# Reordering the DMA transposes on one queue of a fused cross-attention and maxout-FFN kernel

## The chip, the cores and the metric

The kernel runs on one core of a Trainium2 chip. A core has five engines, each with its own in-order instruction queue: PE (TensorE, matrix multiplication), DVE (VectorE), ACT (ScalarE), POOL (GpSimd) and SP (SyncE, which computes nothing and here issues transfers). They wait for one another by semaphores. The metric is the device time of one execution in microseconds; lower is better.

## What is computed

The reference first does a cross-attention between 512 tokens x and 32 states of each of 8 batches and 8 heads, in both directions, and then sends all 8 * (512 + 32) rows through a maxout layer and an output projection:

```python
def _attn_ref(x, state):                      # x: 8,8,512,64   state: 8,8,32,64
    scores = scale * np.matmul(x, state.transpose(0, 1, 3, 2))
    ...                                       # softmax over the 32 states -> a
    xread = np.matmul(a, state)
    scores2 = scale * np.matmul(state, x.transpose(0, 1, 3, 2))
    ...                                       # softmax over the 512 tokens -> a2
    sread = np.matmul(a2, x)
    return np.concatenate([xread, sread], axis=2)

def _moe_ref(x, w1, w2, w3, w_out):           # x: 4352,512   w: 512,768   w_out: 768,512
    h = np.maximum(np.maximum(x @ w1, x @ w2), x @ w3)
    return h @ w_out
```

Inputs and output are float32; the kernel multiplies in bfloat16.

## The kernel before

The work goes batch by batch, 0 to 7, and the stages of several batches are interleaved. For one batch b the names of the stages, which are also the names in the plan below, are these:

- `lx` (line 201): POOL's queue loads x of the batch, 512 KB, into a buffer of its own. `pad` (line 375) copies it on POOL into a padded layout.
- `xtd` (`x_turn_dma`, line 291): SP issues a DMA transpose of x, written to the tile xT.
- `sc` (line 305): PE multiplies xT with the states: the scores. `ex` (line 313): ACT takes the exponential, tile e. `sum` (lines 342 and 344): DVE sums it and takes reciprocals. `wt` (line 349): POOL multiplies e by the reciprocals, tile a, the attention weights.
- `atd` (`a_turn_dma`, line 366): SP issues a DMA transpose of a, written to the tile aT. There are three buffers for aT.
- `sr` (line 391): PE makes the state reads (the sread of the reference). `srs` (line 407): DVE scales them, tile sr. `srt` (`sread_turn`, line 410): SP issues a DMA transpose of them into the batch's own slice of the tile ats. `ap` (`sread_place`, line 415): a copy, on ACT unless the plan says otherwise, from that slice into the tile atp. Only the layer-1 work on the state rows, `l1s`, near the end of the kernel, reads atp.
- `gr`, `gq` (line 427) and `grc`, `gqc` (lines 466 and 469): PE multiplies the states with the three weight matrices, and ACT or DVE copies the result to the tile G. With G, layer 1 is one product with the attention weights.
- `l1 b m` (line 477): PE multiplies aT by G, for slice m (0 to 5) of the 768 hidden units, into three PSUM banks, one for each weight matrix. `m0` (line 492, ACT), `ma` (line 497, DVE) and `mb` (line 505, DVE) take the maximum of the three and so free the three banks.
- `l2 b j` (line 514): PE does the output projection of 128 tokens. `l2c` (line 526): ACT or DVE copies it out of PSUM. `so` (line 548): a queue stores it.

The order is written out by hand. The string PLAN (line 18) is a list of such operations, a function `perform` (line 615) goes through it once and emits the instructions, and each engine runs its own instructions in the order in which they are emitted, each waiting for the data and buffers that it needs. The letters D, A, P and S name the engine or queue. Two operations on different engines that change places in the list change nothing in either engine's own order. BANKS gives the PSUM bank of each operation in the order of the list, for those operations that take one; PLACES gives the buffer of each tile. Of the operations that the change moves, none takes a bank.

In the plan, from batch 2 on, one pass of the loop does the layer 1 of batch b and prepares batch b + 1. SP's queue holds, in the passes of b = 2 to 5, `xtd` of batch b + 2, `srt` of b - 2 and `atd` of b + 1, in this order; the pass of b = 6 has no `xtd`. In the pass of b = 2 that is `xtd 4`, `srt 0`, `atd 3`. `atd` is followed by `ap` of b - 2 on ACT, at the end of the pass, just ahead of `grc`, the copies of the next but one batch's G.

Of the kernel before, what the change touches and what calls it, by code (L numbers as in the profile page):

```python
# [34 lines left out]
    so 0 0 2 P; lx 4; m0 1 5; l2 0 2; ma 1 5; mb 1 5; stp 3 A; l2c 0 2 A; l2 1 0; gq 2 1024 1280; gr 3 0 512;  # L35
    gr 3 1792 2304; l2c 1 0 D; grc 3 1792 2304 D; gqc 2 1024 1280 A; grc 3 0 512 A; atd 2; sr 2; l2 1 1; srs 2;
    sc 3 -; l1 2 0; m0 2 0; ex 3 -; l2c 1 1 D; l2 1 3; ma 2 0; gq 3 1024 1280; so 0 2 4 P; gqc 3 1024 1280 A;
    l2c 1 3 A; gr 3 512 1024; gr 3 1280 1792; mb 2 0; xtd 4; sum 3 -; sr 3; srs 3; l1 2 1; m0 2 1; ma 2 1;
    l1 2 2; m0 2 2; mb 2 1; ma 2 2; l1 2 3; m0 2 3; mb 2 2; srt 0; ma 2 3; l1 2 5; wt 3 - P; m0 2 5; mb 2 3;
    l2 1 2; grc 3 1280 1792 A; grc 3 512 1024 A; ma 2 5; mb 2 5; l2c 1 2 D; l1 2 4; so 1 2 4 P; m0 2 4; ma 2 4;  # L40
    lx 5; mb 2 4; atd 3; ap 0 A; so 1 0 2 P; pad 4; gr 4 1792 2304; gr 4 0 512; grc 4 1792 2304 AD; l2 2 0;
    l2 2 1; grc 4 0 512 D; l2c 2 0 A; l1 3 0; m0 3 0; sc 4 -; ex 4 -; xtd 5; l2c 2 1 D; l2 2 3; ma 3 0;
    gq 4 1024 1280; gr 4 1280 1792; gr 4 512 1024; mb 3 0; sr 4; gqc 4 1024 1280 A; sum 4 -; srs 4; l2c 2 3 A;
    l1 3 1; m0 3 1; ma 3 1; l1 3 2; m0 3 2; mb 3 1; ma 3 2; l1 3 3; m0 3 3; mb 3 2; srt 1; ma 3 3; l1 3 5;
    wt 4 - P; m0 3 5; mb 3 3; l2 2 2; grc 4 1280 1792 A; grc 4 512 1024 A; ma 3 5; mb 3 5; l2c 2 2 D; l1 3 4;
    so 2 2 4 P; m0 3 4; ma 3 4; lx 6; mb 3 4; atd 4; ap 1 A; so 2 0 2 P; pad 5; gr 5 1792 2304; gr 5 0 512;
    grc 5 1792 2304 AD; l2 3 0; l2 3 1; grc 5 0 512 D; l2c 3 0 A; l1 4 0; m0 4 0; sc 5 -; ex 5 -; xtd 6;
    l2c 3 1 D; l2 3 3; ma 4 0; gq 5 1024 1280; gr 5 1280 1792; gr 5 512 1024; mb 4 0; sr 5; gqc 5 1024 1280 A;
    sum 5 -; srs 5; l2c 3 3 A; l1 4 1; m0 4 1; ma 4 1; l1 4 2; m0 4 2; mb 4 1; ma 4 2; l1 4 3; m0 4 3; mb 4 2;
    srt 2; ma 4 3; l1 4 5; wt 5 - P; m0 4 5; mb 4 3; l2 3 2; grc 5 1280 1792 A; grc 5 512 1024 A; ma 4 5;  # L50
    mb 4 5; l2c 3 2 D; l1 4 4; so 3 2 4 P; m0 4 4; ma 4 4; lx 7; mb 4 4; atd 5; ap 2 A; so 3 0 2 P; pad 6;
    gr 6 1792 2304; gr 6 0 512; grc 6 1792 2304 AD; l2 4 0; l2 4 1; grc 6 0 512 D; l2c 4 0 A; l1 5 0; m0 5 0;
    sc 6 -; ex 6 -; xtd 7; l2c 4 1 D; l2 4 3; ma 5 0; gq 6 1024 1280; gr 6 1280 1792; gr 6 512 1024; mb 5 0;
    sr 6; gqc 6 1024 1280 A; sum 6 -; srs 6; l2c 4 3 A; l1 5 1; m0 5 1; ma 5 1; l1 5 2; m0 5 2; mb 5 1; ma 5 2;
    l1 5 3; m0 5 3; mb 5 2; srt 3; ma 5 3; l1 5 5; wt 6 - P; m0 5 5; mb 5 3; l2 4 2; grc 6 1280 1792 A;
    grc 6 512 1024 A; ma 5 5; mb 5 5; l2c 4 2 D; l1 5 4; so 4 2 4 P; m0 5 4; ma 5 4; mb 5 4; atd 6; ap 3 A;
    so 4 0 2 P; pad 7; gr 7 1792 2304; gr 7 0 512; grc 7 1792 2304 AD; l2 5 0; l2 5 1; grc 7 0 512 D; l2c 5 0 A;
    l1 6 0; m0 6 0; sc 7 -; ex 7 -; l2c 5 1 D; l2 5 3; ma 6 0; gq 7 1024 1280; gr 7 1280 1792; gr 7 512 1024;
    mb 6 0; sr 7; gqc 7 1024 1280 A; sum 7 -; srs 7; l2c 5 3 A; l1 6 1; m0 6 1; ma 6 1; l1 6 2; m0 6 2; mb 6 1;
    ma 6 2; l1 6 3; m0 6 3; mb 6 2; srt 4; ma 6 3; l1 6 5; wt 7 - P; m0 6 5; mb 6 3; l2 5 2; grc 7 1280 1792 A;  # L60
    grc 7 512 1024 A; ma 6 5; mb 6 5; l2c 5 2 D; l1 6 4; so 5 2 4 P; m0 6 4; ma 6 4; mb 6 4; atd 7; ap 4 A;
    so 5 0 2 P; srt 6; l1 7 0; srt 7; m0 7 0; l2 6 0; ap 7 D; srt 5; ma 7 0; mb 7 0; l1 7 2; m0 7 2; ap 6 A;
    l2c 6 0 D; ma 7 2; l1 7 3; m0 7 3; ap 5 A; mb 7 2; ma 7 3; l1 7 4; m0 7 4; l2 6 1; l2c 6 1 A; ma 7 4;
    mb 7 4; l1s 0; m0 s 0; l2 6 2; l2c 6 2 A; look; ma s 0; mb s 0; so 6 2 3 S; mb 7 3; l1 7 1; m0 7 1; ma 7 1;
    l1s 2; m0 s 2; mb 7 1; ma s 2; l1 7 5; m0 7 5; mb s 2; ma 7 5; l1s 1; m0 s 1; ma s 1; so 6 0 1 S; mb 7 5;
    l1s 5; m0 s 5; l2p 7 2 384 512; ma s 5; mb s 1; mb s 5; l1s 3; m0 s 3; l2pc 7 2 384 512 A; l2p 7 0 384 512;
    l2p 7 3 256 512; sop 7 2 384 512 P; ma s 3; l2p 7 2 128 384; mb s 3; l2p 7 0 0 128; l2pc 7 0 0 128 A;
    l2pc 7 3 256 512 D; l2p 7 1 0 128; l2pc 7 0 384 512 D; l2p 7 3 0 256; flag; l2pc 7 1 0 128 A;
    l2pc 7 2 128 384 A; l1s 4; m0 s 4; l2 6 3; sop 7 0 0 128 P; ma s 4; sop 7 0 384 512 P; mb s 4;
    l2p s 0 256 512; so 6 1 2 P; l2 s 1; sop 7 3 256 512 A; l2c 6 3 D; l2p 7 2 0 128; sop 7 1 0 128 S;  # L70
    so 6 3 4 A; l2pc 7 3 0 256 D; l2p s 0 0 256; l2pc s 0 256 512 D; sop s 0 256 512 A; l2pc 7 2 0 128 A;
    l2p 7 1 128 384; sop 7 2 0 128 A; l2p 7 0 256 384; l2pc s 0 0 256 A; l2pc 7 1 128 384 A; l2c s 1 D;
    l2p 7 1 384 512; l2p 7 0 128 256; sop 7 3 0 256 S; sop 7 2 128 384 P; l2pc 7 0 256 384 D; sop 7 1 128 384 A;
# [670 lines left out]
```

## Time and profile before

| | us |
|---|---|
| median of 3 runs | 152.40 |
| lowest and highest of them | 151.75, 153.13 |
| the profiled execution, its own time | 153.36 |
| its span, from first to last instruction | 151.6 |

In the profile's rows, a line number and the tile names say which operation a row is: `aT<-a` at L366 is `atd`, `xT<-x` at L291 is `xtd`, `ats<-sr` at L410 is `srt`, `atp<-ats` at L415 is `ap`. A row of a timeline has the start in us, the duration in us, the engine, the line, the operation, the tiles, and the number of instructions merged; in square brackets stand the engine's idle time before it and what ended that. "SPq" rows are the times at which SP's queue issues a transfer; when it lands is told separately, counted from its issue. "PEld" is the loading of weights into PE, which overlaps with its multiplications. A row of busy times in stretches gives, after the stretch, its length, then busy time and number of instructions of PE, PEld, DVE, ACT and POOL, the clock granted to PE, the DMA engines' share and their GB/s.

### The profile page before, as it was taken

The page shows a single profiled execution, that of the slowest core. Times are in us where ns is not written, and L with a number is a line of the kernel's source. Part 1 is how long each engine was busy: PE and PEld are TensorE (multiplying, and loading weights), DVE is VectorE, ACT ScalarE, POOL GpSimd, SP SyncE. Part 2 cuts the span into 40 slices and gives each one's busy share as a digit, 9 for nine tenths or more (in the row PEclk, how much of TensorE's full clock was granted, in tenths as well). Part 3 has the DMA queues.
Part 4 walks back from the last instruction along what each step waited for, and adds up shares of the span by engine and source line. Part 5 has one row for each costly group of instructions (what it writes and reads, how often), then busy time and mean ns, then how long its engine had stood idle before and what let it go on. Part 6 is the DMA issues. An engine that isn't in the chain of part 4 may idle for free.

```text
span 151.6 us, 3618 instructions
## 1 busy us (share of the span) xinstructions
PE 145.2 (96%) x1422; PEld 72.6 (48%) x1422; DVE 118.5 (78%) x202; ACT 83.2 (55%) x144; POOL 56.1 (37%) x78
## 2 busy tenths in 40 slices
PE   6998999999999999899999999999999999999991
PEld 2555443335444443444344435443544446689770
DVE  6488788999967895789978997899779887675443
ACT  3366888966655574466646664666466653332220
POOL 6996911081491508250555055405340200001500
PEclk9999999999999999999999999999999999999999
DMA  4999999959668978996589659965403240300555
GB/s 132 173 182 190 201 232 198 186 113 127 109 145 161 225 152 211 98 215 132 168 100 235 126 163 119 231 129 157 183 4 78 103 191 6 138 0 17 188 202 162
DMA packets 39108, 22.29 MB, mean 147 GB/s; under 512 B 23072, under 2 KB 36896, under 8 KB 39088
## 3 DMA queue, kind: packets, MB, share of 16 engines
q0 software_dynamic: 15872, 13.96, 48.9%
q1 hardware_dynamic: 21632, 6.69, 22.5%
q10 hardware_dynamic: 1584, 1.38, 3.0%
q8 instruction: 12, 0.20, 0.6%
q14 instruction: 8, 0.07, 0.2%
HBM read 15.20 MB, written 8.91 MB: 159 GB/s over the span
## 4 chain that ended last, share of the span: by engine, by line
PE 84%; DMA 8%; POOL 2%; DVE 2%; issue 1%; ACT 1%; POOLq 0%; SPq 0%; DVEq 0%
PE pw L477 46%; PE po L514 22%; PE pg L427 5%; DMA w<-in_moe_w_dram 5%; PE po L532 4%; DMA aT<-a 3%; PE ps L305 2%; PE psr L391 2%; POOL w L217 1%; POOL x L206 1%; PE pgh L427 1%; ACT G L444 1%; PE pt L261 1%; DVE ht L505 0%; DVE t L497 0%
## 5 line engine op out<-in xcount | busy, mean ns | idle before, releaser
L477 PE MATMUL pw<-aT,G 128*128 128x512 bf16 x288 | 66.7, 379 | 0.8 <-DMA aT<-a 0.8
L492 ACT CAST t<-pw 128x512 bf16<-128x512 f32 (+1 forms) x54 | 30.4, 564 | 28.2 <-PE pw L477 25.2
L497 DVE TENSOR_TENSOR t<-t,pw 128x512 bf16<-128x512 bf16 (+1 forms) x54 | 35.3, 655 | 11.0 <-ACT t L492 8.8
L477 PEld LDWEIGHTS <-G 128*128 128x128 bf16 x288 | 27.1, 98 | 33.7 <-issue 3.2
L514 PE MATMUL po<-wout,ht 128*128 128x512 bf16 x168 | 39.7, 379 | 0.0
L505 DVE TENSOR_TENSOR ht<-t,pw 128x512 bf16<-128x512 bf16 x48 | 33.0, 687 | 4.5
L349 POOL TENSOR_TENSOR a<-e,rden 128x1024 bf16<-128x1024 bf16 (+1 forms) x9 | 14.5, 1619 | 27.6 <-ACT osb L526 12.0
L514 PEld LDWEIGHTS <-ht 128*128 128x128 bf16 x168 | 15.4, 98 | 19.0 <-issue 1.7
L548 POOL DMA_DIRECT2D out_dram<-osb x13 | 7.5, 576 | 27.5 <-ACT t L492 27.5
L466 ACT CAST G<-pg 128x1024 bf16<-128x1024 f32 (+1 forms) x17 | 14.7, 901 | 1.5 <-PE pg L427 1.5
L526 ACT COPY osb<-po 128x512 f32<-128x512 f32 x15 | 8.9, 591 | 8.1 <-PE po L514 8.1
L466 DVE CAST G<-pg 128x1024 bf16<-128x1024 f32 (+1 forms) x12 | 11.6, 997 | 1.3 <-ACT G L466 1.2
L526 DVE COPY osb<-po 128x512 f32<-128x512 f32 x14 | 9.6, 687 | 3.6 <-PE po L514 3.5
L375 POOL COPY xp<-x 128x1024 bf16<-128x1024 bf16 x12 | 12.3, 1064 | 0.0
L313 ACT ACTIVATE e<-ps 128x1024 bf16<-128x1024 f32 (+1 forms) x10 | 8.5, 853 | 6.8 <-PE ps L305 6.8
L342 DVE TENSOR_REDUCE seen<-e 128x32 f32<-128x1024 bf16 (+1 forms) x10 | 10.0, 998 | 1.6 <-ACT e L313 1.6
L427 PE MATMUL pg<-w,bd 64*32 64x512 bf16 (+1 forms) x288 | 10.7, 362 | 0.4 <-ACT G L444 0.2
L444 ACT CAST G<-pg 128x768 bf16<-128x768 f32 x10 | 8.0, 810 | 2.7 <-PE pg L427 2.5
L543 POOL DMA_DIRECT2D out_dram<-osb x4 | 2.2, 541 | 19.4 <-ACT osb L537 19.4
L249 PE MATMUL idle<-zero 128*128 128x512 bf16 x18 | 7.4, 503 | 1.8 <-DVE zero L225 1.3
L477 PE MATMUL pw<-atp,w 128*128 128x256 bf16 x72 | 8.7, 272 | 0.0
L217 POOL DMA_DIRECT2D w<-in_moe_w_dram x10 | 7.7, 780 | 0.1
(70 smaller groups left out, 112.7 us busy)
## 6 DMA issues: line engine op xcount, KB each, us to landing
out_dram<-osb POOLq DMA_DIRECT2D x12, 512.0 KB, 3.7
x<-in_x_dram POOLq DMA_DIRECT2D x4, 512.0 KB, 7.5
x<-in_x_dram POOLq DMA_DIRECT2D x7, 256.0 KB, 5.9
w<-in_moe_w_dram POOLq DMA_DIRECT2D x4, 256.0 KB, 7.8
w<-in_moe_w_dram POOLq DMA_DIRECT2D x2, 384.0 KB, 8.0
wout<-in_moe_w_out_dram POOLq DMA_DIRECT2D x1, 768.0 KB, 12.6
out_dram<-osb SPq DMA_DIRECT2D x3, 256.0 KB, 2.4
stf<-in_state_dram ACTq DMA_DIRECT2D x4, 128.0 KB, 5.3
```

Of the source, the lines that this page charges most:

```text
L342: nc.vector.reduce_sum(out=den, in_=parity(e[b], g), axis=AX.X)
L349: times[c](out=parity(a[b], g).rearrange("p j g s n -> p j (g s) n"), in0=parity(e[b], g).rearrange("p j g s n -> p j (g s) n"), in1=rdens ...
L375: nc.gpsimd.tensor_copy(out=xp[b][:, :, :, g * (D + 1):g * (D + 1) + D], in_=v[:, g])
L427: nc.tensor.matmul(p(s, g), bd(b, 2 * s + g)[64 * g:64 * g + 64, g, :], f(w_sb[64 * g:64 * g + 64, s]), start=True, stop=True, tile_positi ...
L444: copier[c[g]](out=G[b][:, g:h, :, m * 128:m * 128 + 128], in_=p[:, g:h, 0:384].rearrange("p g (i f) -> p g i f", i=3))
L466: copier[c[g]](out=v[:, g:h], in_=p[:, g:h, 0:c1 - c0])
L477: nc.tensor.matmul(pw[i][:, 0:n], lhs(i, k), rhs(k), start=(k == 0), stop=(k == nk - 1))
L492: nc.scalar.copy(out=t0s[b, m][:, 0:n], in_=open_ps["l", b, m][0][:, 0:n])
L497: nc.vector.tensor_max(t1s[b, m][:, 0:n], t0s.pop((b, m))[:, 0:n], open_ps["l", b, m][1][:, 0:n])
L505: nc.vector.tensor_max(ht[b][:, m, :], t1s.pop((b, m))[:, 0:n], open_ps.pop(("l", b, m))[2][:, 0:n])
L514: nc.tensor.matmul(p, ht[b][:, m, tokens(b, j)], wout_sb[:, m, :], start=(m == 0), stop=(m == NM - 1))
L526: copier[c[i]](out=o[:, j, i * w:i * w + w], in_=p[:, i * w:i * w + w])
```

## The change

The same 595 operations stand in the list before and after, in another order; nothing else is edited. The list is wrapped anew, so the diff touches many lines; with one operation a line its core is this:

```diff
 mb 2 0
+sum 3 -
+wt 3 - P
+atd 3
 xtd 4
-sum 3 -
+srt 0
 sr 3
...
 mb 2 2
-srt 0
 ma 2 3
 l1 2 5
-wt 3 - P
 m0 2 5
...
 mb 2 4
-atd 3
-ap 0 A
 so 1 0 2 P
...
 mb 3 2
-srt 1
 ma 3 3
...
 atd 4
-ap 1 A
+srt 1
+ap 0 A
 so 2 0 2 P
...
 mb 4 2
-srt 2
 ma 4 3
...
 atd 5
-ap 2 A
+srt 2
+ap 1 A
 so 3 0 2 P
...
 mb 5 2
-srt 3
 ma 5 3
...
 atd 6
-ap 3 A
+srt 3
+ap 2 A
 so 4 0 2 P
...
 atd 7
+ap 3 A
 ap 4 A
```

In the pass of b = 2, SP's queue now holds `atd 3`, `xtd 4`, `srt 0`; in the passes of b = 3 to 5, `xtd`, `atd`, `srt`. In the pass of b = 6 the queue holds `srt 4` and `atd 7` as before. On ACT, `ap 0` to `ap 3` each move to the end of the next pass, so that the pass of b = 2 has none and the pass of b = 6 has two, `ap 3` and `ap 4`.

More of the change, by code (lines that the diff above doesn't have):

```diff
@@ L37 @@
     sc 3 -; l1 2 0; m0 2 0; ex 3 -; l2c 1 1 D; l2 1 3; ma 2 0; gq 3 1024 1280; so 0 2 4 P; gqc 3 1024 1280 A;
[L38 to L70, printed above, removed]
+    l2c 1 3 A; gr 3 512 1024; gr 3 1280 1792; mb 2 0; sum 3 -; wt 3 - P; atd 3; xtd 4; srt 0; sr 3; srs 3;
@@ new lines @@
+    l1 2 1; m0 2 1; ma 2 1; l1 2 2; m0 2 2; mb 2 1; ma 2 2; l1 2 3; m0 2 3; mb 2 2; ma 2 3; l1 2 5; m0 2 5;
+    mb 2 3; l2 1 2; grc 3 1280 1792 A; grc 3 512 1024 A; ma 2 5; mb 2 5; l2c 1 2 D; l1 2 4; so 1 2 4 P; m0 2 4;
+    ma 2 4; lx 5; mb 2 4; so 1 0 2 P; pad 4; gr 4 1792 2304; gr 4 0 512; grc 4 1792 2304 AD; l2 2 0; l2 2 1;
+    grc 4 0 512 D; l2c 2 0 A; l1 3 0; m0 3 0; sc 4 -; ex 4 -; xtd 5; l2c 2 1 D; l2 2 3; ma 3 0; gq 4 1024 1280;
+    gr 4 1280 1792; gr 4 512 1024; mb 3 0; sr 4; gqc 4 1024 1280 A; sum 4 -; srs 4; l2c 2 3 A; l1 3 1; m0 3 1;
@@ new lines @@
+    ma 3 1; l1 3 2; m0 3 2; mb 3 1; ma 3 2; l1 3 3; m0 3 3; mb 3 2; ma 3 3; l1 3 5; wt 4 - P; m0 3 5; mb 3 3;
+    l2 2 2; grc 4 1280 1792 A; grc 4 512 1024 A; ma 3 5; mb 3 5; l2c 2 2 D; l1 3 4; so 2 2 4 P; m0 3 4; ma 3 4;
+    lx 6; mb 3 4; atd 4; srt 1; ap 0 A; so 2 0 2 P; pad 5; gr 5 1792 2304; gr 5 0 512; grc 5 1792 2304 AD;
+    l2 3 0; l2 3 1; grc 5 0 512 D; l2c 3 0 A; l1 4 0; m0 4 0; sc 5 -; ex 5 -; xtd 6; l2c 3 1 D; l2 3 3; ma 4 0;
+    gq 5 1024 1280; gr 5 1280 1792; gr 5 512 1024; mb 4 0; sr 5; gqc 5 1024 1280 A; sum 5 -; srs 5; l2c 3 3 A;
@@ new lines @@
+    l1 4 1; m0 4 1; ma 4 1; l1 4 2; m0 4 2; mb 4 1; ma 4 2; l1 4 3; m0 4 3; mb 4 2; ma 4 3; l1 4 5; wt 5 - P;
+    m0 4 5; mb 4 3; l2 3 2; grc 5 1280 1792 A; grc 5 512 1024 A; ma 4 5; mb 4 5; l2c 3 2 D; l1 4 4; so 3 2 4 P;
+    m0 4 4; ma 4 4; lx 7; mb 4 4; atd 5; srt 2; ap 1 A; so 3 0 2 P; pad 6; gr 6 1792 2304; gr 6 0 512;
+    grc 6 1792 2304 AD; l2 4 0; l2 4 1; grc 6 0 512 D; l2c 4 0 A; l1 5 0; m0 5 0; sc 6 -; ex 6 -; xtd 7;
+    l2c 4 1 D; l2 4 3; ma 5 0; gq 6 1024 1280; gr 6 1280 1792; gr 6 512 1024; mb 5 0; sr 6; gqc 6 1024 1280 A;
@@ new lines @@
+    sum 6 -; srs 6; l2c 4 3 A; l1 5 1; m0 5 1; ma 5 1; l1 5 2; m0 5 2; mb 5 1; ma 5 2; l1 5 3; m0 5 3; mb 5 2;
+    ma 5 3; l1 5 5; wt 6 - P; m0 5 5; mb 5 3; l2 4 2; grc 6 1280 1792 A; grc 6 512 1024 A; ma 5 5; mb 5 5;
+    l2c 4 2 D; l1 5 4; so 4 2 4 P; m0 5 4; ma 5 4; mb 5 4; atd 6; srt 3; ap 2 A; so 4 0 2 P; pad 7;
+    gr 7 1792 2304; gr 7 0 512; grc 7 1792 2304 AD; l2 5 0; l2 5 1; grc 7 0 512 D; l2c 5 0 A; l1 6 0; m0 6 0;
+    sc 7 -; ex 7 -; l2c 5 1 D; l2 5 3; ma 6 0; gq 7 1024 1280; gr 7 1280 1792; gr 7 512 1024; mb 6 0; sr 7;
@@ new lines @@
+    gqc 7 1024 1280 A; sum 7 -; srs 7; l2c 5 3 A; l1 6 1; m0 6 1; ma 6 1; l1 6 2; m0 6 2; mb 6 1; ma 6 2;
+    l1 6 3; m0 6 3; mb 6 2; srt 4; ma 6 3; l1 6 5; wt 7 - P; m0 6 5; mb 6 3; l2 5 2; grc 7 1280 1792 A;
+    grc 7 512 1024 A; ma 6 5; mb 6 5; l2c 5 2 D; l1 6 4; so 5 2 4 P; m0 6 4; ma 6 4; mb 6 4; atd 7; ap 3 A;
+    ap 4 A; so 5 0 2 P; srt 6; l1 7 0; srt 7; m0 7 0; l2 6 0; ap 7 D; srt 5; ma 7 0; mb 7 0; l1 7 2; m0 7 2;
+    ap 6 A; l2c 6 0 D; ma 7 2; l1 7 3; m0 7 3; ap 5 A; mb 7 2; ma 7 3; l1 7 4; m0 7 4; l2 6 1; l2c 6 1 A;
@@ new lines @@
+    ma 7 4; mb 7 4; l1s 0; m0 s 0; l2 6 2; l2c 6 2 A; look; ma s 0; mb s 0; so 6 2 3 S; mb 7 3; l1 7 1; m0 7 1;
+    ma 7 1; l1s 2; m0 s 2; mb 7 1; ma s 2; l1 7 5; m0 7 5; mb s 2; ma 7 5; l1s 1; m0 s 1; ma s 1; so 6 0 1 S;
+    mb 7 5; l1s 5; m0 s 5; l2p 7 2 384 512; ma s 5; mb s 1; mb s 5; l1s 3; m0 s 3; l2pc 7 2 384 512 A;
+    l2p 7 0 384 512; l2p 7 3 256 512; sop 7 2 384 512 P; ma s 3; l2p 7 2 128 384; mb s 3; l2p 7 0 0 128;
+    l2pc 7 0 0 128 A; l2pc 7 3 256 512 D; l2p 7 1 0 128; l2pc 7 0 384 512 D; l2p 7 3 0 256; flag;
@@ L71 @@
+    l2pc 7 1 0 128 A; l2pc 7 2 128 384 A; l1s 4; m0 s 4; l2 6 3; sop 7 0 0 128 P; ma s 4; sop 7 0 384 512 P;
+    mb s 4; l2p s 0 256 512; so 6 1 2 P; l2 s 1; sop 7 3 256 512 A; l2c 6 3 D; l2p 7 2 0 128; sop 7 1 0 128 S;
     so 6 3 4 A; l2pc 7 3 0 256 D; l2p s 0 0 256; l2pc s 0 256 512 D; sop s 0 256 512 A; l2pc 7 2 0 128 A;
```

## The prediction

> **What bounds the kernel now.** I read first the page's busy shares, then where the busiest engine idles, then the wait behind that idle time, and last the queue that issued what it waited for.
>
> ```profile
> span 151.6 us, 3618 instructions
> PE 145.2 (96%) x1422; PEld 72.6 (48%) x1422; DVE 118.5 (78%) x202; ACT 83.2 (55%) x144; POOL 56.1 (37%) x78
> ```
> ```profile
> 16.00:60.00 44.00, 44.00 (x435) 19.05 (x434) 36.69 (x58) 30.03 (x50) 18.47 (x26) 1.00 0.97 170
> 60.00:62.00 2.00, 1.23 (x7) 0.47 (x6) 2.00 (x3) 0.31 (x2) 1.58 (x2) 1.00 0.79 88
> 62.00:148.00 86.00, 86.00 (x785) 45.50 (x784) 67.25 (x118) 44.46 (x81) 22.89 (x28) 1.00 0.57 132
> ```
>
> The second view gives, for each stretch, its length and then PE's busy time: 44.00 of 44.00 us, 1.23 of 2.00, 86.00 of 86.00, always at granted clock 1.00. So from 16 us to the end PE sets the time, and it idles once, for 0.77 us, between 60 and 62. An edit of order can take that away; all else it can do is to put a new hole into PE. The row of PE there, and the chain of work around it, name what it waited for:
>
> ```profile
> 57.23 0.63 PE L427 MATMUL pg<-w,bd 64*32 64x512 bf16 x16
> 57.78 2.76 PE L514 MATMUL po<-wout,ht 128*128 128x512 bf16 x12
> 61.31 1.46 PE L477 MATMUL pw<-aT,G 128*128 128x512 bf16 x6 [0.77 <-DMA aT<-a]
> 62.61 0.63 PE L305 MATMUL ps<-bd,xT 128*128 128x64 bf16 x16
> ```
> ```profile
> 56.41 4.87 DMA aT<-a
> ```
>
> These are the first layer-1 matmuls of batch 3 (l1 3 0), waiting for the turned weights aT of batch 3 (atd 3), issued at 56.41 and landed 4.87 us later. They could have been issued sooner: POOL had the weights done at 50.02 + 1.90 = 51.92, while SP first sat at the head of its queue on xtd 4 (waiting for x of batch 4), then issued it and srt 0:
>
> ```profile
> 40.14 1.91 POOL L349 TENSOR_TENSOR a<-e,rden 128x1024 bf16<-128x1024 bf16 x1 [5.48 <-ACT t L492]
> 50.02 1.90 POOL L349 TENSOR_TENSOR a<-e,rden 128x1024 bf16<-128x1024 bf16 x1 [3.93 <-PE pw L477]
> 42.08 1.23 SPq L366 DMA_TRANSPOSE aT<-a  x1
> 52.67 1.73 SPq L291 DMA_TRANSPOSE xT<-x  x1
> 54.52 1.77 SPq L410 DMA_TRANSPOSE ats<-sr  x1
> 56.41 1.80 SPq L366 DMA_TRANSPOSE aT<-a  x1
> 66.33 2.79 SPq L291 DMA_TRANSPOSE xT<-x  x1
> 69.17 1.23 SPq L410 DMA_TRANSPOSE ats<-sr  x1
> 70.51 1.24 SPq L366 DMA_TRANSPOSE aT<-a  x1
> ```
>
> **The change part by part.** Nothing is added or removed: the same operations stand in another order, and none changes place against others on PE, DVE or POOL. Only SP and ACT see a new order.
>
> *wt 3 and sum 3 earlier in the list.* On POOL wt 3 still stands between the stores so 0 2 4 and so 1 2 4, on DVE sum 3 still precedes srs 3. Cost nothing: wt 3 ends at 51.92 as before.
>
> *atd 3 ahead of xtd 4 and srt 0.* SP is free from 43.31 (42.08 + 1.23), so atd 3 goes out at about 51.95, as the one at 42.08 went 0.03 us after its own weights (40.14 + 1.91 = 42.05). The landings of all six of these transfers are (minimum, median, maximum):
>
> ```profile
> DMA to landing us min/median/max: 2.7/2.7/4.9
> ```
>
> So aT is there between 54.7 and 56.9. The price of the hole is best read against the same place one batch later, which has no wait:
>
> ```profile
> 73.41 0.62 PE L427 MATMUL pg<-w,bd 64*32 64x512 bf16 x16
> 76.56 1.46 PE L477 MATMUL pw<-aT,G 128*128 128x512 bf16 x6
> 77.86 0.63 PE L305 MATMUL ps<-bd,xT 128*128 128x64 bf16 x16
> ```
>
> From the start of the G matmuls to the start of l1: 76.56 - 73.41 = 3.15 us there, 61.31 - 57.23 = 4.08 here. The difference is 0.93, a little over the labelled 0.77 because the ends of matmuls are modelled. I take 0.93, since starts are recorded; 0.77 is the lower bound of the hole. Without it l1 3 0 starts at 57.23 + 3.15 = 60.38.
>
> What is late next there? Its three PSUM banks are freed by ma 2 4 and mb 2 4 on DVE and by the copy l2c 2 0 on ACT:
>
> ```profile
> 57.88 0.69 DVE L505 TENSOR_TENSOR ht<-t,pw 128x512 bf16<-128x512 bf16 x1
> 58.88 0.48 ACT L415 COPY atp<-ats 128x128 bf16<-128x128 bf16 x1 [1.83 <-DMA ats<-sr]
> 59.10 0.68 ACT L466 CAST G<-pg 128x512 bf16<-128x512 f32 x1
> 59.69 0.57 ACT L526 COPY osb<-po 128x512 f32<-128x512 f32 x1
> ```
>
> mb 2 4 ends at 58.57 and l2c 2 0 at 60.26, both ahead of 60.38 even as they stand; and ACT, which today waits 1.83 us for ats of batch 0 in front of that copy (ap 0), loses this wait, as ap 0 moves a batch on. So the whole 0.93 is taken, if aT comes in time.
>
> *xtd 4 and srt 0 behind atd 3.* SP issues xtd 4 at 51.95 + 1.25 + 0.05 = 53.25 and not at 52.67, then srt 0 at 55 to 56, by the 1.73 to 2.79 that the rows above give an xT issue. The landings around it, medians from issue in the stretch 48 to 62 us:
>
> ```profile
> out_dram<-osb POOLq DMA_DIRECT2D x2, 512.0 KB, 6.1
> x<-in_x_dram POOLq DMA_DIRECT2D x1, 512.0 KB, 8.2
> xT<-x SPq DMA_TRANSPOSE x1, 5.9
> ats<-sr SPq DMA_TRANSPOSE x1, 4.3
> ```
>
> ```profile
> DMA to landing us min/median/max: 4.2/4.8/6.5
> ```
> ```profile
> 44.65 0.90 POOL L201 DMA_DIRECT2D x<-in_x_dram  x1
> 57.44 0.61 POOL L548 DMA_DIRECT2D out_dram<-osb  x1 [5.51 <-ACT t L492]
> 58.05 0.92 POOL L201 DMA_DIRECT2D x<-in_x_dram  x1
> ```
> ```profile
> x<-in_x_dram POOLq DMA_DIRECT2D x1, 512.0 KB, 7.9
> ```
>
> The single landing row is that of all six xT; the last row is the x of batch 4, issued at 44.65, so landed at 52.55, just ahead of 52.67. So xT 4, by the 5.9 of its own row, lands at about 59.15. Its reader, the scores sc 4, now comes at 60.38 + 1.30 = 61.68 (1.30 is 62.61 - 61.31, and 77.86 - 76.56): 2.5 us of cover. Even if atd 3's packets held the x of batch 4 back by 0.7, to 53.25, SP would not notice. Cost nothing; without the cover, every microsecond after 61.68 is one of PE's. [...]
>
> ```profile
> 66.14 1.91 POOL L349 TENSOR_TENSOR a<-e,rden 128x1024 bf16<-128x1024 bf16 x1 [4.55 <-ACT osb L526]
> ```
>
> *srt 1 to srt 3 behind atd 4 to atd 6.* atd 4 goes out at about 69.17 and not at 70.51. Its weights are ready by then, at 66.14 + 1.91 = 68.05, and today, by the median of 2.7, aT 4 lands at 70.51 + 2.7 = 73.2 for l1 4 0 at 76.56: 3.3 us to spare already. Gain nothing, loss nothing; srt 1 is 1.3 us later and its reader ap 1 a whole batch (15 us) later.
>
> *The copies ap.* In batches 3 to 5 ACT's slot holds another ap of the same 0.48 us, so nothing changes. The last one holds two, ap 3 and ap 4:
>
> ```profile
> 118.88 0.48 ACT L415 COPY atp<-ats 128x128 bf16<-128x128 bf16 x1
> 119.69 0.58 ACT L492 CAST t<-pw 128x512 bf16<-128x512 f32 x1 [0.33 <-PE pw L477]
> ```
> ```profile
> 120.36 1.46 PE L514 MATMUL po<-wout,ht 128*128 128x512 bf16 x6
> ```
>
> The cast at 119.69 is m0 7 0, and it frees the bank of l2 6 0, PE's row at 120.36: it ends at 120.27, so there is hardly 0.1 us of slack. ACT idles 0.33 ahead of it and gets 0.48 more: 0.15 late at most. But 58.88 to 59.10 above shows ACT starting the next operation 0.22 after an ap, less than 0.33, which makes it 0. I take 0, nearest to the row of the same operation, and keep 0.15 as the bound.
>
> **Sum.** The profiled execution took 153.36 us, 1.76 of them outside the span of 151.6. 153.36 - 0.93 + 0 = 152.43. It stands 0.96 above the median of the three runs shown (152.40), so on the median: 152.40 - 0.93 = 151.47, **151.5**. With the bounds (0.77 - 0.15 = 0.62) it is 151.5 to 151.8.
>
> **The rivals.**
> *The gain doesn't show* (152.4). The hole rests on a landing of 4.87, when the median is 2.7. With a landing of 3.9 at the same issue, l1 3 0 would have started on time. Timed runs may have no such hole, and then the change does nothing. For: five of the six batches have none. Against: in one chain xT, ats and aT all landed late there (5.9, 4.3, 4.9), so it isn't one transfer's chance.
>
> *More than the hole* (150.8). In timed runs the hole may be larger: the longest xT landing in the trace is 6.5 against this one's 5.9, and a chain 0.6 later gives 0.93 + 0.6 = 1.53. Against: the profiled execution is itself the longer one.
>
> *Slower: the wait goes over to sc 4* (153.3). Place: PE at 61.68, the scores waiting for xT 4. It decides when xT 4 needs over 61.68 - 53.25 = 8.4 us; it costs more than the hole did from 9.4. If its completion had to stand behind the store issued at 57.44, it would come at 57.44 + 6.1 = 63.54, 1.86 late: 152.43 + 1.86 = 154.29, on the median 153.3. For: xT 4 starts 0.6 later, and both transfers are then in flight with it. Against: aT 3 today was issued at 56.41, had the same store and load beside it, and landed at 61.28, not at 63.54; the longest xT landing is 6.5, which gives 59.75.
>
> **How the numbers follow.** The forecast case gets 0.68, no visible gain 0.16, more than the hole 0.09, the wait for sc 4 0.07. Three runs of before lie between 151.75 and 153.13, so a median carries some 0.5 either way: the forecast's own range is 150.9 to 152.1, and with the neighbours 150.6 to 152.7. About 1% (1.5 us) is what a measurement of this kernel tells from no change. Faster than 150.9: half of the large-hole case and a quarter of the forecast's spread, 0.22. Slower than 153.9: a part of the sc 4 case and what I don't see, 0.08. Within: 0.70.
>
> **What would show it.** In the changed profile: SP issues aT 3 at about 51.95 and xT 4 at about 53.25; PE's l1 3 0 starts 3.15 after its G matmuls, with no wait; ACT has no wait for ats; PE stays full from 16 to 147, and the span is 150.7. Wrong it would be if PE waits at sc 4, if l2 6 0 starts late behind two ap, or if any other hole opens; and the size is wrong if the timed runs had no hole to lose.

## The result, and the profile after

| | before | changed |
|---|---|---|
| median of 22 runs each, us | 153.15 | 152.28 |
| lowest and highest, us | 151.75, 154.36 | 151.69, 152.94 |
| profiled execution, us | 153.36 | 152.38 |
| its span, us | 151.6 | 150.5 |

The ratio of the times is 0.9956, with a 95% interval of 0.9936 to 0.9975: 0.44% faster, which at 153.15 us is 0.67 us (0.38 to 0.98). The ratio leaves out the two runs of the kernel before that lie more than 1.5% above its fastest, 154.05 and 154.36; the medians, which have them in, differ by 0.87. The lowest runs of both kernels are within 0.1 us of each other; what the change takes away is the upper part of the runs: 16 of 22 lie above 152.6 before, 2 of 22 after.

In the changed kernel's profile, first PE's busy time by stretches (columns as before), then the rows of PE around l1 3 0:

```profile
16.00:60.00 44.00, 44.00 (x435) 19.06 (x434) 37.92 (x58) 29.99 (x49) 18.47 (x26) 1.00 0.96 172
60.00:62.00 2.00, 2.00 (x24) 1.11 (x22) 1.36 (x3) 0.59 (x1) 1.47 (x2) 1.00 0.65 42
62.00:146.50 84.50, 84.50 (x768) 44.52 (x765) 66.12 (x116) 44.26 (x81) 22.91 (x28) 1.00 0.58 132
```
```profile
57.12 0.63 PE L427 MATMUL pg<-w,bd 64*32 64x512 bf16 x16
57.68 2.76 PE L514 MATMUL po<-wout,ht 128*128 128x512 bf16 x12
60.28 1.46 PE L477 MATMUL pw<-aT,G 128*128 128x512 bf16 x6
61.57 0.63 PE L305 MATMUL ps<-bd,xT 128*128 128x64 bf16 x16
```

PE is full from 16 to 146.5 us, and l1 3 0 starts 60.28 - 57.12 = 3.16 after the G matmuls, where it was 4.08. The timeline of SP, ACT and DVE in this pass, and the landings counted from issue:

```profile
51.86 1.35 SPq L366 DMA_TRANSPOSE aT<-a  x1
53.32 1.98 SPq L291 DMA_TRANSPOSE xT<-x  x1
55.40 1.54 SPq L410 DMA_TRANSPOSE ats<-sr  x1
57.60 0.59 ACT L466 CAST G<-pg 128x512 bf16<-128x512 f32 x1 [0.65 <-PE pg L427]
59.18 0.59 ACT L526 COPY osb<-po 128x512 f32<-128x512 f32 x1 [1.00 <-PE po L514]
```
```profile
aT<-a SPq DMA_TRANSPOSE x1, 3.2
xT<-x SPq DMA_TRANSPOSE x1, 6.0
ats<-sr SPq DMA_TRANSPOSE x1, 4.1
```

aT 3 lands at 51.86 + 3.2 = 55.1, five us before its use; xT 4 at 53.32 + 6.0 = 59.3, 2.2 us before sc 4; and ACT, without ap 0, copies G at 57.60 instead of 59.10.

### The profile page after: what moved, and what is told of

It reads as the page before. It is cut to its first block, busy times and chain, and to the rows that moved or that the text cites. A ratio compares the mean times of both kernels' runs of the same rounds, so it can differ in the third digit from the quotient of the medians.

```text
span 150.5 us, 3618 instructions
## 1 busy us (share of the span) xinstructions
PE 145.1 (96%) x1422; PEld 72.8 (48%) x1422; DVE 118.0 (78%) x202; ACT 83.2 (55%) x144; POOL 56.1 (37%) x78
## 4 chain that ended last, share of the span: by engine, by line
PE 88%; DMA 5%; POOL 3%; issue 1%; DVE 1%; ACT 1%; POOLq 0%
PE pw L477 47%; PE po L514 25%; PE pg L427 6%; DMA w<-in_moe_w_dram 5%; PE po L532 4%; PE ps L305 2%; PE psr L391 2%; POOL w L217 1%; POOL x L206 1%; PE pgh L427 1%; ACT G L444 1%; PE pt L261 1%; DVE held L593 0%; PE idle L591 0%; PE pat L358 0%
```

## The experiments

Theories at the start: the gain is PE's hole, opened by the order on SP's queue (queue theory); or it is ACT's lost wait for ats (copies theory); or the order in the later passes counts. Each kernel below is compared with runs of the kernel before on the same chip.

**The whole change again**, beside its parts:

> The changed kernel once more, beside the three parts of it, so that all four share their runs of the kernel before. Queue theory (the gain is the hole that PE had in front of l1 3 0, because atd 3 stood behind xtd 4 and srt 0 on SP's queue): time ratio to before about 0.995, PE full from 16 us to 147 us, l1 3 0 some 3.15 us after its G matmuls.

Measured: 0.9958 (0.9928 to 0.9988), median 152.18; no wait of PE at l1 3 0.

**The queue's order alone.** In the pass of b = 2 the diff is that of the change, without the lines of ap:

```diff
 mb 2 0
+sum 3 -
+wt 3 - P
+atd 3
 xtd 4
-sum 3 -
+srt 0
...
-atd 3
 ap 0 A
```

> Only the pass of b = 2 on SP's queue: atd 3, xtd 4, srt 0, with all copies ap and all later passes as before. Queue theory: the hole is gone, ratio about 0.995 as with the whole change; ap 0 on ACT now waits longer for ats (srt 0 goes out at about 55.4 and lands at about 59.5), by some 2.4 us, but the bank that ACT frees behind it is needed only at 61.2, so PE loses at most 0.2 us to it. Copies theory (the gain is ACT's lost wait for ats in ap 0): the hole stays or a new one opens, ratio 1.00 or above.

Measured: 1.0025 (0.9994 to 1.0057), median 153.11, lowest 152.70. Nothing gained, against the queue theory as I had it. The timeline shows why:

```profile
59.35 0.48 ACT L415 COPY atp<-ats 128x128 bf16<-128x128 bf16 x1 [2.62 <-DMA ats<-sr]
59.58 0.68 ACT L466 CAST G<-pg 128x512 bf16<-128x512 f32 x1
60.06 1.46 PE L477 MATMUL pw<-aT,G 128*128 128x512 bf16 x6
60.28 1.82 DVE L466 CAST G<-pg 128x512 bf16<-128x512 f32 x2 [2.04 <-ACT G L466]
62.02 0.68 DVE L526 COPY osb<-po 128x512 f32<-128x512 f32 x1
62.76 1.46 PE L514 MATMUL po<-wout,ht 128*128 128x512 bf16 x6 [0.78 <-DVE osb L526]
```

l1 3 0 starts on time, at 60.06. But srt 0 now goes out last, ap 0 waits 2.62 us for it on ACT, the copy of G behind it is late, DVE's copies of G wait for that, and behind them stands l2c 2 1, which frees the bank of PE's l2 2 3. PE gets a hole of 0.78 there in place of the 0.77 at l1. Moving ap 0 out of the pass is therefore half of the change.

**The copies alone** (ap 0 to ap 3 one pass later, SP's queue untouched):

> Only the copies ap 0 to ap 3 one pass later, SP's queue as before. Queue theory: aT 3 still lands at about 61.3, PE's hole of 0.77 us (0.93 from start to start) stays, ratio 1.00; ACT's wait of 1.83 us for ats goes without any effect on the time. Copies theory: ratio about 0.995 and no hole.

Measured: 0.9991 (0.9950 to 1.0033). PE's row, in the same columns:

```profile
61.45 1.46 PE L477 MATMUL pw<-aT,G 128*128 128x512 bf16 x6 [1.30 <-DMA aT<-a]
```

The hole stays; the copies theory falls. Neither half does anything alone.

**The later passes alone**, measured twice:

```diff
-srt 1
...
 atd 4
-ap 1 A
+srt 1
...
 atd 5
-ap 2 A
+srt 2
+ap 1 A
...
```

> Only the passes of b = 3 to 5: srt behind atd, and the copies ap 1 to ap 3 one pass later; the pass of b = 2 as before. Queue theory: aT was 3.3 us early in these passes already, so the hole at 60 us stays and nothing is gained, ratio 1.00. A theory that the order of every pass counts: ratio about 0.996 to 0.998.

Measured: 0.9966 (0.9931 to 1.0002), and no hole in the profile, though the pass of b = 2 was untouched. So it was run again:

> The later passes alone once more, since the first measurement (0.9966, interval 0.9931 to 1.0002) left it open. Two-part theory: the pass of b = 2 is that of the kernel before, so the hole comes and goes from run to run as there, ratio 1.00, runs from 151.8 to 154.4. Theory that the later passes count: ratio 0.996 again.

Measured: 1.0003 (0.9963 to 1.0043), with the hole in the profile. These two executions of one program are the best witness of the case. SP's row and the landing of aT 3 in the first, then in the second, with its hole:

```profile
55.82 1.81 SPq L366 DMA_TRANSPOSE aT<-a  x1
```
```profile
aT<-a SPq DMA_TRANSPOSE x1, 3.3
```
```profile
56.31 1.78 SPq L366 DMA_TRANSPOSE aT<-a  x1
61.14 1.45 PE L477 MATMUL pw<-aT,G 128*128 128x512 bf16 x6 [0.65 <-DMA aT<-a]
```
```profile
aT<-a SPq DMA_TRANSPOSE x1, 4.8
```

Issued 0.5 us later, aT 3 lands 2 us later. What comes between is POOL's store so 1 2 4. Its issue, and its own landing, in the first, the second, and the kernel before:

```profile
57.26 0.61 POOL L548 DMA_DIRECT2D out_dram<-osb  x1 [5.51 <-ACT t L492]
```
```profile
out_dram<-osb POOLq DMA_DIRECT2D x1, 512.0 KB, 3.4
```
```profile
57.38 0.61 POOL L548 DMA_DIRECT2D out_dram<-osb  x1 [5.51 <-ACT t L492]
```
```profile
out_dram<-osb POOLq DMA_DIRECT2D x1, 512.0 KB, 3.5
```
```profile
out_dram<-osb POOLq DMA_DIRECT2D x1, 512.0 KB, 3.7
```

In the second, the store lands at 57.38 + 3.5 = 60.9 and aT 3 at 61.1; in the kernel before, the store at 57.44 + 3.7 = 61.1 and aT 3 at 61.3; in the copies-alone run, 61.2 and 61.4. In the first, aT 3 is down at 59.1 and the store only at 60.7. So there are two outcomes: SP's issue of aT 3 is done early enough and it lands in 3.3 us, or the store gets in with it and it lands just behind the store. The issue ends at 57.63 in the first case, 0.37 after the store's start, and at 58.09, 58.21 and 57.99 in the others, 0.7 to 1.0 after it: the point lies between. Which of the two comes depends on when x of batch 4 lands, since xtd 4 and srt 0 wait for it ahead of atd 3: at 52.0 in the first execution, at 52.4 in the second.

What was late can be seen in the packets that the DMA engines moved. In these rows q1 is SP's queue and q0 POOL's; the number of packets and the MB follow (the share of time behind them isn't used here). First execution, SP's queue from 56.9 to 58.7 us, then both queues from 58.7 to 60.7:

```profile
q1 hardware_dynamic: 1066, 0.26, 109.4%
```
```profile
q0 software_dynamic: 155, 0.47, 83.6%
```

Second execution, SP's queue from 57.4 to 59.2, then both from 59.2 to 61.2:

```profile
q1 hardware_dynamic: 1034, 0.26, 104.7%
```
```profile
q0 software_dynamic: 139, 0.42, 65.9%
q1 hardware_dynamic: 32, 0.00, 0.9%
```

The 0.26 MB of aT 3 (128x1024 in bfloat16) have been moved by 58.7 in the first and by 59.2 in the second. After that SP's queue has nothing more in the first; in the second 32 packets of next to no data follow, among the data of the store. So the data of aT 3 were no more than 0.5 us later, as its issue was. What came late were these last packets and the landing; what the packets carry, the traces don't tell. The kernel before is the same: 0.26 MB between 57.5 and 59.3, and 32 packets of 0.00 MB between 59.3 and 61.3 (by shorter stretches, between 60.3 and 60.7, with the landing at 61.3).

This splits the runs. Of 104 runs of the kernel before in four series 100 stayed under 156 us, and 65 of these lie above 152.6 (in a fifth series 5 of 8); of the 34 runs of the changed kernel, 2. Only one execution in each series of a kernel's runs has a profile. Where SP's pass of b = 2 and the loads are as before, the three profiled executions above 152.6 have the hole (153.36, 153.21 and 152.97 us), and the two below have none (152.16, the first one here, and 151.85 with the stores later). That all other runs split in the same way is taken from their times alone.

**The first pass with its copies, later passes' queue as before:**

> The change without its later passes: atd 3, xtd 4, srt 0 in the pass of b = 2 and all copies ap one pass later, but srt 1 to srt 3 ahead of atd 4 to atd 6 as before. Two-part theory (order on SP's queue takes away the wait for aT, the copy ap 0 out of the pass takes away the chain that would follow it over ACT and DVE; the later passes do nothing): PE full from 16 to 147 us, ratio about 0.995, as with the whole change. Theory that the later passes count: ratio about 0.998, a part of the gain is missing.

Measured: 0.9982 (0.9949 to 1.0015), median 152.35, 11 of 12 runs at 151.83 to 152.52 and one at 156.01, no wait of PE in the profile. The ratio doesn't decide; runs and profile are those of the whole change. I take the later passes to be worth nothing measurable.

**The stores later.** The kernel before, with POOL kept busy ahead of them:

```diff
+pad 4
+pad 4
+pad 4
 so 1 2 4 P
...
 lx 5
...
 so 1 0 2 P
-pad 4
```

> The kernel before, with POOL's padding of batch 4 done three times (twice more than needed, the same values) ahead of the store so 1 2 4, the load of x of batch 5 and the store so 1 0 2, which so go out at about 59.2 us instead of 57.4; SP's order as before. Contention theory (aT 3, issued at 56.4, lands after 4.9 us instead of some 3 because the store and the load come onto the DMA engines with it): aT 3 lands by about 59.7 and the hole is gone in every run, ratio about 0.995, narrow. Pure queue theory (the landing takes 4.9 there whatever else runs): aT 3 lands at 61.3, the hole of 0.8 us stays, ratio 1.00. Side effect: x of batch 5 lands some 1.8 us later, which the pass of b = 3 can hide (3.3 us).

Measured: 0.9971 (0.9939 to 1.0003), median 152.41, highest 152.83: the interval touches 1, but the runs are about as narrow as the changed kernel's, with SP's order untouched; 3 of 12 lie above 152.6, where 65 of 100 do without the paddings. The store went out at 57.85, not at 59.2 (POOL could start the paddings at 51.8), and aT 3, issued from 55.64 to 57.43, landed in 3.3 us. In this execution it would probably have been early enough anyway: in the others the store goes out 7.4 us after wt 3 starts, which gives 57.1 here, an estimate, and 0.3 between it and the end of the issue. So it is the runs, not the profile, that speak for the race with the store, and for SP's order as only one way to win it.

**Only past the state reads.** The changed kernel with `xtd 4` put back ahead of `atd 3`:

> The changed kernel with xtd 4 put back ahead of atd 3: SP's order in the pass of b = 2 is xtd 4, atd 3, srt 0, so the weights still stand behind the queue head that waits for x of batch 4, and pass only srt 0. They go out at about 54.5 us, some 2.9 us before the store that POOL issues at 57.4. Theory that the landing decides by whether aT 3 goes out ahead of that store and the load behind it: aT 3 lands by about 58, no hole, ratio about 0.995 and narrow runs as with the whole change. Theory that the wait behind x of batch 4 is what costs: a hole or a scatter of runs up to 154 remains, ratio about 1.00.

Measured: 0.9947 (0.9921 to 0.9973), median 152.19, no hole. SP's rows, and the landing of aT 3:

```profile
52.46 1.69 SPq L291 DMA_TRANSPOSE xT<-x  x1
54.26 1.97 SPq L366 DMA_TRANSPOSE aT<-a  x1
56.34 1.63 SPq L410 DMA_TRANSPOSE ats<-sr  x1
```
```profile
aT<-a SPq DMA_TRANSPOSE x1, 5.1
```

It lands at 59.4, 0.8 behind xT 4 (52.46 + 6.1 = 58.6): later than with the whole change, but in time. Passing srt 0 is enough here; waiting behind the x of batch 4 was no cost in itself.

**One more transpose ahead.** The other way: aT 3 goes out later. Copies later as above, and on SP:

```diff
+def sread_turn_more(b):
+    nc.sync.dma_start_transpose(out=more, in_=srs[b].rearrange("p g d -> p (g d)"))
...
 mb 2 2
+srx 0
 srt 0
```

> The other way: copies ap one pass later, SP's queue as before, and one more DMA transpose of the size of srt (of the state reads of batch 0, to a tile of its own that nothing reads) between xtd 4 and srt 0, so that atd 3 goes out some 1.8 us later, at about 58.2 us, behind POOL's store (57.4) and about with its load of x of batch 5 (58.0). Queue theory with a fixed landing of 4.9 us: aT 3 lands at about 63.1, the hole is 2.7 us, ratio about 1.012 to 1.015. Contention theory: a transpose that goes out behind the load lands with it, as aT 2 did in the run with the earlier load (8.6 us), so at about 66; the hole is 5 to 6 us, ratio 1.03 to 1.04, and no run without a hole.

Measured: 1.0421 (1.0370 to 1.0473), 6 runs. The profiled execution took 162.18 us, where the median is 160.19. Issue rows of POOL's load and of aT 3 (the line numbers are four or less higher in this kernel), the landings, PE's wait, and the stretch behind it:

```profile
57.90 0.91 POOL L202 DMA_DIRECT2D x<-in_x_dram  x1
58.17 1.61 SPq L367 DMA_TRANSPOSE aT<-a  x1
```
```profile
x<-in_x_dram POOLq DMA_DIRECT2D x1, 512.0 KB, 9.6
aT<-a SPq DMA_TRANSPOSE x1, 10.5
```
```profile
68.70 2.72 PE L481 MATMUL pw<-aT,G 128*128 128x512 bf16 x6 [8.31 <-DMA aT<-a]
68.70:72.00 3.30, 3.30 (x23) 1.63 (x23) 1.22 (x2) 0.59 (x1) 0.00 (x0) 0.56 0.90 169
```

1.8 us later on SP are 8.3 us of waiting on PE: aT 3 lands at 68.7, 1.2 behind the load (57.90 + 9.6 = 67.5) and together with the store so 1 0 2, which POOL issued at 58.79 (58.79 + 9.9 = 68.7), while SP was still issuing aT 3. Here the data came late too: the 0.26 MB of aT 3 moved only between 61.7 and 68, beside the load and that store. Behind the wait the granted clock was 0.56, and six matmuls of l1 took 2.72 us instead of 1.46. The fixed landing of 4.9 falls; the contention theory had the direction, but with a hole of 5 to 6 us and a ratio up to 1.04 too small a size.

**The load of x of batch 5 behind the padding,** on top of that kernel:

> The kernel with one more transpose ahead of atd 3, as in the run before, but with POOL's load of x of batch 5 moved behind the store so 1 0 2 and the padding of batch 4, to about 61 us; the store so 1 2 4 stays at about 57.4, so 1 0 2 comes at about 58. aT 3 still goes out at about 58.2, so behind the stores but ahead of the load. If it is the load that holds the landing (as the load at 42.15 us did with aT 2): aT 3 lands after some 5 us, at about 63, hole 2.5 to 3 us, ratio 1.01 to 1.02. If the stores hold it: it lands after 8 to 10 us as before, ratio 1.03 to 1.045. Side effect: x of batch 5 lands some 3 us later, at about 69 to 70, which may cost the pass of b = 3 up to 1 us.

Measured: 1.0359 (1.0315 to 1.0403), 4 runs; aT 3, issued at 57.19, lands after 6.3 us at 63.5, PE waits 3.7. The landing and the hole lie between those of the two expectations. The two stores, issued at 56.73 and 57.3, land at 59.9 and 62.8, and aT 3 0.7 behind the second; its 0.26 MB moved between 59.6 and 63. So aT 3 lands late with only stores issued ahead of it too, 6.3 us where aT 2 of the kernel before took 2.7, and its landing is some 4 us shorter than with the load ahead. How much of these 4 us is the load's isn't settled, since aT 3 also went out 1 us sooner.

**x of batch 4 loaded earlier,** by moving `lx 4` to just behind `wt 2`:

> The kernel before, with the load of x of batch 4 three POOL operations earlier (right behind wt 2, at about 42.0 us instead of 44.65), SP's order as before. Theory that the hole is a transfer stuck behind a waiting queue head: x of batch 4 lands by about 49, xtd 4 and srt 0 are gone before the weights are ready at 52, atd 3 goes out at about 52 and there is no hole, nor does ap 0 wait: ratio about 0.995, and the runs as narrow as with the change. Rival (the order of the three transposes itself is what counts): hole as before, ratio 1.00. The loads of x of batch 3 may be disturbed by the earlier load; then a new wait shows at sc 3 around 45 us.

Measured: 1.0459 (1.0413 to 1.0506). The experiment ran into the same thing one pass earlier, since the load now went out beside aT 2:

```profile
42.15 0.95 POOL L201 DMA_DIRECT2D x<-in_x_dram  x1
42.23 1.23 SPq L366 DMA_TRANSPOSE aT<-a  x1
50.90 2.72 PE L477 MATMUL pw<-aT,G 128*128 128x512 bf16 x6 [4.98 <-DMA aT<-a]
```

aT 2, issued 0.08 us behind the load, landed after 8.6 us (50.8), the load after 8.5 (50.65). In the kernel before, where the load came 2.6 us behind the transpose, it landed in 2.7. Again the data weren't late: the 0.26 MB of aT 2 moved between 43.3 and 45.1, and 32 packets of 0.00 MB came after that. So this run says nothing on the wait behind x of batch 4, which the run with `xtd 4` put back answers; it shows what a transpose that went out behind a load took: 8.6 us, against 2.7 ahead of it.

## Why the prediction was wrong on the time, and where it was right

- **Direction, place and profiled execution: right.** The hole at l1 3 0 was the only one and is gone; 152.43 was worked out for the profiled execution, 152.38 came. The starts of PE gave the right price (0.92 regained, 0.93 worked out).
- **The time: wrong.** The forecast was 151.5, with a range of its own of 150.9 to 152.1 (150.6 to 152.7 with its neighbours); the median is 152.28. The step that failed is the last of the sum, 152.40 - 0.93: the hole of the profiled execution was taken off the median of three runs as if each run had it. The profiled execution (153.36) had the hole, and 0.96 of difference to the median, about the size of the hole, stood in the sum and was passed over. The runs showed that 152.40 is by its time a run without the hole, like 151.75 and unlike 153.13, so there was nothing in it to take off. The median of 22 runs of the kernel before is 153.15, and 153.15 - 0.93 = 152.22 is near the measured 152.28. So the price of the hole was right, and the time from which it was taken was 0.75 too low.
- **The gain over all runs** is smaller than 0.93 for the same reason: 65 of 100 runs lie above 152.6, and 0.65 * 0.93 = 0.60, an estimate, is near the measured 0.67. My rival "the gain doesn't show" had the right idea and the wrong form: it isn't one case or the other for the kernel, but for each run.
- **"About 1% is what a measurement tells": wrong.** I took the spread of three runs (151.75 to 153.13) for noise, and gave 0.70 to no visible change. By the split of the runs, most of that spread was the hole coming and going; 20 of the changed kernel's 22 runs lie within 151.7 to 152.4, and 22 of each side tell 0.44% from no change.
- **The copies: right by luck.** "What is late next?" was answered for the three banks of l1 3 0 alone, and the move of ap 0 was booked as a side gain. With the new queue order it is a condition: left in place, it costs the 0.78 us that the queue saves. I should have followed ACT's delay on to DVE's copies and to the bank of l2 2 3. The expectation of the queue-alone run failed by the same step.
- **The slower rival: the evidence against it was misread.** I argued that aT 3 at 61.28 hadn't waited for the store, which I had land at 63.54 by the 6.1 of a row that is the median of two stores. The store at 57.44 alone landed after 3.7, at 61.1, and aT 3 only behind it, at 61.3. The other two profiles with the hole have the same: aT 3 landed 0.1 to 0.2 us behind the store, and in the two whose packets are counted above its data had been moved by 59.2 and 59.3. With the earlier load, aT 2 landed 0.2 behind the load, its data moved by 45.1. Where aT 3 went out behind the load or between the two stores, its data came late as well (moved between 61.7 and 68, and between 59.6 and 63); what held the data there no run shows. That xT 4 would have to stand behind the store was my assumption, and no run shows it: in the changed kernel its issue was over at 55.3, two us ahead of the store (57.33), and it landed in 6.0 us, against 5.9 before.
- **The last two ap: right.** m0 7 0 starts 118.64 - 116.71 = 1.93 after the start of PE's pair of l1, before 119.69 - 117.77 = 1.92, and l2 6 0 2.59 after it in both. PE's pair of l1 before, then the rows of the changed kernel:

```profile
117.77 2.75 PE L477 MATMUL pw<-aT,G 128*128 128x512 bf16 x12
```
```profile
116.71 2.75 PE L477 MATMUL pw<-aT,G 128*128 128x512 bf16 x12
119.30 1.46 PE L514 MATMUL po<-wout,ht 128*128 128x512 bf16 x6
```
```profile
117.83 0.77 ACT L415 COPY atp<-ats 128x128 bf16<-128x128 bf16 x2
118.64 0.59 ACT L492 CAST t<-pw 128x512 bf16<-128x512 f32 x1
```

## What to carry to other kernels

A wait that the trace shows once can be a race that some runs win: look at the spread of the runs and at several profiles, price it by how often it is lost, and take its price off a time that has it in. Where a small transfer that an engine waits for runs beside large stores and loads of another queue, it should be issued clearly ahead of them; the cost of coming late was here not the lateness but the landing of what got ahead (issued 0.5 us later, aT 3 landed 2 us later, 0.2 behind the store; issued 1.8 us later, behind the load, it kept PE waiting 8.3). And when an operation is put last in a queue, whatever reads its result must move back with it, or the wait only changes its engine (here from 0.77 us of PE at l1 3 0 to 2.62 us of ACT at ap 0, and 0.78 of PE at l2 2 3).

## What the runs showed of the hardware

A DMA transpose (128x1024 in bfloat16) that landed in 2.7 us while POOL's queue moved nothing took 8.6 and 10.5 us when issued 0.08 and 0.27 us behind a load of 512 KB from that queue. In two runs its data had been moved long before it counted as landed: by 59.2 with a landing at 61.1 behind a store, by 45.1 with a landing at 50.8 behind a load. The granted clock of PE was 1.00 in the stretches around a wait of 1.30 us (60 to 62 us and 62 to 147, copies alone). Behind waits of 3.68, 4.98 and 8.31 us it was 0.68 (64 to 68, with the load behind the padding), 0.50 (51 to 54, x of batch 4 earlier) and 0.56 (68.7 to 72, one more transpose ahead), and the same six matmuls took 2.72 us instead of 1.46. From which length of wait between 1.30 and 3.68 us on the clock falls, no run here shows.
